# Second denominators next to the last kv product, output tiles 0 and 1 interleaved around them

## The chip, the cores and the metric

One core of a Trainium2 chip. The metric is the device time of one launch in microseconds (us).

Profiles name the engines in short: PE is TensorE (PEld its weight loads), DVE is VectorE, ACT is ScalarE, POOL is GpSimd and SP is SyncE, which issues most transfers. A bank here is one 128 x 512 f32 tile of the pools in PSUM, where this kernel's matmuls put their results.

## The reference, cut to what matters

```python
q, k, v = split(x @ wqkv)                        # 2048 rows, 32 heads of 32
pq, pk = phi(q), phi(k)                          # phi: t+1 where t > 0, else exp(t)
kv  = einsum("bhsd,bhse->bhde", pk, v)
z   = sum of pk over s
num = pq @ kv ;  den = pq @ z + 1e-6
a   = (num / den) @ wo
b   = x + (an expert's output, added to one row)
out = g * a + (1 - g) * b                        # g = sigmoid(x . gate_w)
```

The kernel multiplies kv with wo first (`m_sb`, a 1024 x 1024 matrix). It divides pq by its denominator in place, and then one product per output tile, pq times m_sb, gives a. Sixteen tiles of 128 rows are written.

## The kernel before

TensorE (`pe`) works in three array shapes at the place in question. Projections and output products use 128*128, the kv product with wo (`unit_M`, tiles `pm`) uses 32*32, and the denominators (`den_group`, tile `dps`) use 128*32.

```python
M_AFTER = {3: (0, 0), 6: (0, 1), 9: (1, 0), 12: (1, 1)}    # unit_M behind these projections
NORM_PER_T = [2, 3, 0, 2, 2, 2, 2, 2, 2, 2, 2, 1, 0, 0, 0, 0]

def den_group(pair):                     # denominators of 1024 rows: blocks j = 2*pair, 2*pair + 1
    pool, tag = (ps_work, "w") if pair == 0 else (ps_den, "d")
    dps = pool.tile([P, 512], F32, tag=tag, name="dps")
    ...                                  # 16 matmuls, lhsT = zc[:, g, :], rhs = pq_all[:, g, block j]
    act.activation(dn[:], dps[:], ACTF.Identity, bias=eps_t[:, 0:1])
    dve.reciprocal(rd[:], dn[:])
    for hh in range(4):                  # to rdp, half on SyncE's queue, half on GpSimd's
        eng = nc.sync if hh % 2 == 0 else nc.gpsimd
        eng.dma_start(out=rdp[pair][32 * hh : 32 * hh + 16, :], in_=rd[hh : P : 8, :])

def norm_step(n):                        # one of 32 normalisations: 8 g for each of 4 blocks j
    ...
    dve.stream_shuffle(rb[:], rd[:], [8 * (j % 2) + g] * 32)     # rb has four buffers
    nc.gpsimd.tensor_tensor(sl, sl, rb[:], op=ALU.mult)          # sl: pq_all, in place

def unit_M(hf, nh):                      # kv times wo, a quarter of m_sb
    pm = four_banks("pm")                # three banks of ps_den, one of ps_ffn
    ...                                  # 16 matmuls of 32*32, all side by side
    for r in range(4):
        eng = dve.tensor_copy if r == 3 else act.copy
        eng(m_sb[:, 4 * hf + r, 512 * nh : 512 * nh + 512], pm[r][:])
...
for i in range(len(q_units)):            # the last 13 projection units
    unit_Q(*q_units.popleft())
    if i in M_AFTER: unit_M(*M_AFTER[i])
    if i >= 3: norm_step(1)
phq.close()
for t in range(NT):                      # 16 output tiles, two column halves each
    ...                                  # load xt, xg = xt * (1 - gate) on ACT
    for c0, cw in cols:
        ...                              # 8 matmuls into ps (ps_work, four buffers)
        dve.scalar_tensor_tensor(ot[...], ps[...], gate[...], xg[...], op0=ALU.mult, op1=ALU.add)
    ...                                  # store ot
    if t == 0:
        rdB = den_group(1); normalise(rdB, 2); normalise(rdB, 3)
    norm_step(NORM_PER_T[t])
```

Of the kernel before, what the change touches and what calls it, by code (L numbers as in the profile page):

```python
# [13 lines left out]
BF = mybir.dt.bfloat16  # L14
F32 = mybir.dt.float32
I32 = mybir.dt.int32
U32 = mybir.dt.uint32
ALU = mybir.AluOpType
ACTF = mybir.ActivationFunctionType
# [3 lines left out]
P = 128  # L23
S = 2048
D = 1024
F = 3584
NT = S // P
KC = D // P
NG = D // P
# [7 lines left out]
KV_BEHIND = {(6, 3): 6}  # L37
FLUSH_AFTER = {(10, 2)}
ROW_STEPS = {4: (0, 1, 0, 1, 0, 1), 5: (0, 1, 0, 1, 1), 6: (0, 0, 0, 0, 1), 7: (0, 1, 1, 0, 1), 8: (0, 1, 0, 1, 1), 9: (1,)}
M_AFTER = {3: (0, 0), 6: (0, 1), 9: (1, 0), 12: (1, 1)}  # L40
DOWN_STEPS = {10: (0, 0, 0, 1, 1, 1), 11: (1, 1, 1, 1, 1), 12: (1, 1, 1, 1, 1), 13: (1, 1, 1, 1, 1), 14: (1, 1, 1, 1, 1), 15: (1, 1, 1, 1, 1)}
FFN_DEPTH = 10
NORM_PER_T = [2, 3, 0, 2, 2, 2, 2, 2, 2, 2, 2, 1, 0, 0, 0, 0]
# [3 lines left out]
def kernel(  # L47
# [13 lines left out]
    nc = tc.nc  # L61
    x2d = A_x.rearrange("b s d -> (b s) d")
    out2d = out.rearrange("b s d -> (b s) d")
# [6 lines left out]
    ps_work = ctx.enter_context(tc.tile_pool(name="ps_work", bufs=4, space=PSUM))  # L70
# [5 lines left out]
    strict = [True]  # L76
    strict_dve = [False]

    def in_order(engine, names, own=(False,)):
        last = [None]  # L80

        def wrap(fn):
            def call(*a, **k):
                inst = fn(*a, **k)  # L84
                if last[0] is not None and (strict[0] or own[0]):
                    tc.add_manual_dep(inst.ins, last[0].ins.name, NOSYNC, reason="program order on this engine")
                last[0] = inst
                return inst

            return call  # L90

        return SimpleNamespace(**{n: wrap(getattr(engine, n)) for n in names})

    pe = in_order(nc.tensor, ["matmul", "transpose"])
    dve = in_order(nc.vector, ["memset", "tensor_copy", "tensor_scalar", "tensor_scalar_add", "tensor_tensor", "scalar_tensor_tensor",
                               "reciprocal", "max", "max_index", "tensor_reduce", "stream_shuffle"], strict_dve)
    sp = in_order(nc.sync, ["dma_start", "dma_start_transpose"])
    act = in_order(nc.scalar, ["activation", "copy"])

    pq_all = keep.tile([P, NG, S], BF)  # L100
    gate = keep.tile([P, NT], F32)
    omg = keep.tile([P, NT], F32)
# [3 lines left out]
    xp = dram.tile([S, D], BF, name="xp")  # L106
# [144 lines left out]
    def unit_Q(g, j):  # L251
        ps = ps_work.tile([P, 512], F32, tag="w")
        for c in range(KC):
            pe.matmul(ps[:], lhsT=wq[:, c, g * P : (g + 1) * P], rhs=xT[:, c, 512 * j : 512 * j + 512],
                             start=(c == 0), stop=(c == KC - 1))
        phi_evac(ps[:], pq_all[:, g, 512 * j : 512 * j + 512])
# [337 lines left out]
    pb = ctx.enter_context(tc.tile_pool(name="pb", bufs=1))  # L594
    m_sb = pb.tile([P, NG, D], BF)
# [10 lines left out]
    ps_den = ctx.enter_context(tc.tile_pool(name="ps_den", bufs=3, space=PSUM))  # L606

    def den_group(pair):
        pool, tag = (ps_work, "w") if pair == 0 else (ps_den, "d")
        dps = pool.tile([P, 512], F32, tag=tag, name="dps")  # L610
        strict[0] = True
        for g0 in range(4):
            for jj in range(2):
                for g1 in range(2):
                    g = 4 * g1 + g0
                    j = 2 * pair + jj
                    q = 2 * jj + g1
                    pe.matmul(dps[32 * q : 32 * q + 32, :], lhsT=zc[:, g, :], rhs=pq_all[:, g, 512 * j : 512 * j + 512],
                                     start=(g0 == 0), stop=(g0 == 3), tile_position=(0, 32 * q))
        strict[0] = False  # L620
        dn = tmpb.tile([P, 512], F32, tag="dn")
        act.activation(dn[:], dps[:], ACTF.Identity, bias=eps_t[:, 0:1])
        rd = tmpb.tile([P, 512], F32, tag="rd")
        dve.reciprocal(rd[:], dn[:])
        for hh in range(4):
            eng = nc.sync if hh % 2 == 0 else nc.gpsimd
            eng.dma_start(out=rdp[pair][32 * hh : 32 * hh + 16, :], in_=rd[hh : P : 8, :])
        return rdp[pair]
# [3 lines left out]
    def normalise(rd, j):  # L632
        for g in range(NG):
            norm_units.append((rd, g, j))

    def norm_step(n):
        for _ in range(n):
            if not norm_units:
                return
            rd, g, j = norm_units.popleft()  # L640
            rb = tmpb.tile([P, 512], F32, tag="rb", bufs=4)
            dve.stream_shuffle(rb[:], rd[:], [8 * (j % 2) + g] * 32)
            sl = pq_all[:, g, 512 * j : 512 * j + 512]
            nc.gpsimd.tensor_tensor(sl, sl, rb[:], op=ALU.mult)  # L644

    def four_banks(name):
        banks = [ps_den.tile([P, 512], F32, tag="d", name=f"{name}{r}") for r in range(3)]
        banks.append(ps_ffn.tile([P, 512], F32, tag="f", name=f"{name}3"))
        return banks
# [14 lines left out]
    def unit_M(hf, nh):  # L664
        pm = four_banks("pm")
        for c in range(4):
            for r in range(4):
                pe.matmul(pm[r][32 * c : 32 * c + 32, :], lhsT=kvT[32 * r : 32 * r + 32, hf, c, :],
                          rhs=wo[2 * hf + c // 2][0][32 * r : 32 * r + 32, 1024 * (c % 2) + 512 * nh : 1024 * (c % 2) + 512 * nh + 512],
                          start=True, stop=True, tile_position=(32 * r, 32 * c))  # L670
# [4 lines that stand above are left out]
    rdA = den_group(0)  # L675
    strict[0] = True
    unit_kvT()
    strict[0] = False
    normalise(rdA, 0)
    normalise(rdA, 1)  # L680
    strict[0] = True
    for i in range(len(q_units)):
        unit_Q(*q_units.popleft())
        if i in M_AFTER:
            unit_M(*M_AFTER[i])
        if i >= 3:
            norm_step(1)
    strict[0] = False
    phq.close()

    fin = ctx.enter_context(tc.tile_pool(name="fin", bufs=3))
    for t in range(NT):
        xt = fin.tile([P, D], BF, tag="x3")
        nc.sync.dma_start(out=xt[:], in_=xp[t * P : (t + 1) * P, :])
        xg = fin.tile([P, D], F32, tag="xg3")
        strict[0] = True
        act.activation(xg[:], xt[:], ACTF.Copy, scale=omg[:, t : t + 1])
        strict[0] = False
        ot = fin.tile([P, D], BF, tag="o3")
        cols = [(0, 512), (512, 512)] if t < NT - 1 else [(0, 512), (512, 288), (800, 224)]  # L700
        for c0, cw in cols:
            ps = ps_work.tile([P, 512], F32, tag="w")
            for g in range(NG):
                pe.matmul(ps[:, 0:cw], lhsT=pq_all[:, g, t * P : (t + 1) * P], rhs=m_sb[:, g, c0 : c0 + cw],
                                 start=(g == 0), stop=(g == NG - 1))
            dve.scalar_tensor_tensor(ot[:, c0 : c0 + cw], ps[:, 0:cw], gate[:, t : t + 1],
                                           xg[:, c0 : c0 + cw], op0=ALU.mult, op1=ALU.add)
            if t == NT - 1:
                nc.sync.dma_start(out=out2d[t * P : (t + 1) * P, c0 : c0 + cw], in_=ot[:, c0 : c0 + cw])
        if t < NT - 1:  # L710
            nc.sync.dma_start(out=out2d[t * P : (t + 1) * P, :], in_=ot[:])
        if t == 0:
            rdB = den_group(1)
            normalise(rdB, 2)
            normalise(rdB, 3)
        norm_step(NORM_PER_T[t])


# [28 lines left out]
```

## Time and profile before

| | before |
|---|---|
| time, median of 6 runs | 248.58 us (248.30 to 248.77) |
| profiled span | 246.6 us |
| TensorE busy | 241.8 us (98%) |
| first projection behind the third `pm` to the last matmul, start to start | 61.92 us |
| start of the last matmul to the end of the span | 3.82 us |

The chain of waits that ended last, in order of time (start, duration, engine, tile), finishes like this in the kernel before:

```profile
186.22 0.36 PE pm L84 x16
186.59 3.56 PE ps L84 x16
190.15 0.98 PE dps L84 x16
191.12 51.94 PE ps L84 x248
243.06 0.02 issue
243.09 0.45 DVE ot L84
```

Each row begins where the one above ends. TensorE is the chain, and the last output evacuation on VectorE (DVE) closes it.

### The profile page before, as it was taken

How to read it: one execution, taken by the hardware profiler on the slowest of the kernel's cores; microseconds unless marked ns; L12 is line 12 of the kernel's file. 1: busy time of each engine (PE TensorE's matmuls, PEld its weight loads, DVE VectorE, ACT ScalarE, POOL GpSimd, SP SyncE). 2: the span in 40 equal slices, each digit the busy share in tenths (PEclk: the TensorE clock that was granted, in tenths of full speed). 3: DMA queues.
4: the chain of work that ended last, by engine and by line, in shares of the span. 5: the costliest groups of instructions: out<-in, count | busy, mean ns of one | idle time of the engine just before them, and what ended most of it. 6: DMA issues, size and time to landing. Idle time of an engine off the chain costs nothing.

```text
span 246.6 us, 4896 instructions
## 1 busy us (share of the span) xinstructions
PE 241.8 (98%) x1926; PEld 124.6 (51%) x1926; DVE 172.6 (70%) x264; ACT 127.5 (52%) x215; POOL 52.6 (21%) x100
## 2 busy tenths in 40 slices
PE   8999999999999999999999999999999999999994
PEld 4466756654565554554555555444443444444442
DVE  1053124379975899835999999996789999954442
ACT  3095343355554565545576455668887633333300
POOL 6000000400000000000003400101666689950000
PEclk9999999999999999999999999999999999999999
DMA  6999994399968994499549690000003664464122
GB/s 215 341 239 196 274 390 139 108 350 335 265 192 251 353 314 120 146 319 386 188 157 535 212 287 16 3 4 21 0 3 128 202 185 147 153 190 166 48 85 86
DMA packets 46311, 47.78 MB, mean 194 GB/s; under 512 B 16776, under 2 KB 35472, under 8 KB 46224
## 3 DMA queue, kind: packets, MB, share of 16 engines
q1 hardware_dynamic: 45648, 46.28, 60.7%
q0 software_dynamic: 608, 1.19, 1.6%
q8 instruction: 15, 0.25, 0.4%
q14 instruction: 8, 0.07, 0.1%
q10 hardware_dynamic: 32, 0.00, 0.0%
HBM read 39.33 MB, written 8.39 MB: 194 GB/s over the span
## 4 chain that ended last, share of the span: by engine, by line
PE 96%; DMA 2%; SPq 1%; DVE 0%; issue 0%
PE ps L84 89%; PE first L84 3%; PE kvacc L84 2%; DMA wkv<-in_A_wqkv_dram 2%; PE dps L84 1%; PE red L84 1%; PE pm L84 1%; SPq L84 1%; PE yps L84 0%; DVE ot L84 0%; PE pt L84 0%; PE hps L84 0%; PE rps L84 0%; PE xs_ps L84 0%
## 5 line engine op out<-in xcount | busy, mean ns | idle before, releaser
L84 PE MATMUL ps<-wkv,xT 128*128 128x352 bf16 (+2 forms) x608 | 106.5, 334 | 0.0
L84 PEld LDWEIGHTS <-xT 128*128 128x128 bf16 x640 | 62.2, 98 | 49.7 <-issue 0.9
L84 ACT ACTIVATE u<-ps 128x512 f32<-128x512 f32 x60 | 35.9, 598 | 45.4 <-PE ps L84 45.2
L84 PE MATMUL ps<-xT,wq 128*128 128x512 bf16 x256 | 58.1, 379 | 0.0
L84 PE MATMUL ps<-m_sb,pq_all 128*128 128x512 bf16 (+2 forms) x264 | 55.6, 373 | 0.0
L84 ACT ACTIVATE e<-u 128x512 f32<-128x512 f32 x64 | 40.3, 630 | 2.0
L84 PEld LDWEIGHTS <-pq_all 128*128 128x128 bf16 x264 | 25.7, 98 | 29.9 <-issue 0.7
L644 POOL TENSOR_TENSOR pq_all<-pq_all,rb 128x512 bf16<-128x512 bf16 x32 | 36.4, 1166 | 12.1 <-DVE rb L84 11.7
L84 PEld LDWEIGHTS <-wq 128*128 128x128 bf16 x256 | 24.6, 98 | 28.1 <-issue 0.7
L84 DVE SCALAR_TENSOR_TENSOR gacc<-wt,hcol,gacc 128x1024 f32<-128x1024 bf16 x27 | 34.5, 1278 | 0.4
L84 DVE SCALAR_TENSOR_TENSOR ot<-ps,gate,xg 128x512 bf16<-128x512 f32 (+2 forms) x33 | 24.0, 736 | 14.2 <-PE ps L84 14.1
L84 DVE SCALAR_TENSOR_TENSOR gacc<-wt,xs_f,gacc 128x2048 f32<-128x2048 bf16 x14 | 32.8, 2345 | 0.2
L84 ACT ACTIVATE xg<-xt,omg 128x1024 f32<-128x1024 bf16 x16 | 18.1, 1146 | 26.9 <-DVE ot L84 25.9
L84 DVE SCALAR_TENSOR_TENSOR pq_all<-ps,e 128x512 bf16<-128x512 f32 x32 | 21.9, 687 | 11.7 <-ACT e L84 11.7
L84 DVE SCALAR_TENSOR_TENSOR pk<-ps,e 128x512 bf16<-128x512 f32 x28 | 18.9, 684 | 10.0 <-ACT e L84 10.0
L84 DVE STREAM_SHUFFLE rb<-rdp 128x512 f32<-128x512 f32 x32 | 22.7, 747 | 0.0
L84 ACT CAST vt<-ps 128x352 bf16<-128x352 f32 x32 | 14.3, 453 | 11.4 <-PE ps L84 11.1
L214 POOL MEMSET vt<- 128x22 bf16 x16 | 3.8, 445 | 56.1 <-PE kvacc L84 55.9
L480 POOL DMA_DIRECT2D wt<-in_A_wo_dram x8 | 4.3, 542 | 32.1 <-PE ps L84 29.5
L84 ACT CAST vc<-ps 128x320 bf16<-128x320 f32 x16 | 6.5, 428 | 7.3 <-PE ps L84 7.3
L84 DVE COPY rg<-ps 128x2 f32<-128x2 f32 x16 | 2.5, 159 | 10.2 <-ACT vc L84 10.1
L356 POOL DMA_DIRECT2D xs<-in_A_x_dram x1 | 0.7, 711 | 39.3 <-DVE sig L84 39.3
(100 smaller groups left out, 93.9 us busy)
## 6 DMA issues: line engine op xcount, KB each, us to landing
wt<-in_B_w_down_dram SPq DMA_DIRECT2D x14, 512.0 KB, 4.0
wt<-in_B_w_gate_dram SPq DMA_DIRECT2D x8, 512.0 KB, 7.5
wt<-in_B_w_up_dram SPq DMA_DIRECT2D x8, 512.0 KB, 7.2
xt<-xp SPq DMA_DIRECT2D x16, 256.0 KB, 2.6
out_dram<-ot SPq DMA_DIRECT2D x15, 256.0 KB, 2.0
wt<-in_B_w_gate_dram SPq DMA_DIRECT2D x8, 384.0 KB, 7.1
wt<-in_B_w_up_dram SPq DMA_DIRECT2D x8, 384.0 KB, 6.8
wkv<-in_A_wqkv_dram SPq DMA_DIRECT2D x8, 256.0 KB, 4.3
```

Of the source, the lines that this page charges most:

```text
L84: inst = fn(*a, **k)
L214: nc.gpsimd.memset(vt_t[t][:, :, 32:33], 1.0)
L356: nc.gpsimd.dma_start(out=xs8[:], in_=x2d[bass.ds(idx_val, 1), :].rearrange("o (c p) -> (o c) p", p=P))
L480: ld = eng.dma_start(out=wt[32 * r : 32 * r + 32, :].rearrange("p (c n) -> p c n", c=2), in_=wo_v[k // 2, r][:, 2 * (k % 2) : 2 * (k % 2) ...
L644: nc.gpsimd.tensor_tensor(sl, sl, rb[:], op=ALU.mult)
```

## The change

Its intent is to save a change of array shape on TensorE. The denominators of the second half move right behind the last `unit_M`, so that the two small shapes are adjacent. Tile 0's first output half runs ahead of both, to give VectorE time for the last projection unit, which those denominators need. Tile 1's first half goes between the halves of tile 0. For this, tile 0's x is loaded and scaled earlier, into buffers of its own, and the denominators use a bank of `ps_work`.

```diff
-M_AFTER = {3: (0, 0), 6: (0, 1), 9: (1, 0), 12: (1, 1)}
+M_AFTER = {3: (0, 0), 6: (0, 1), 9: (1, 0)}
 ...
-        pool, tag = (ps_work, "w") if pair == 0 else (ps_den, "d")
-        dps = pool.tile([P, 512], F32, tag=tag, name="dps")
+        dps = ps_work.tile([P, 512], F32, tag="w", name="dps")
 ...
+    xt0 = final_load(0, pb, 1)
     for i in range(len(q_units)):
         unit_Q(*q_units.popleft())
         ...
+        if i == 10:
+            final_scale(0, xt0)
+    final_cols(0, 0, 512)
+    unit_M(1, 1)
+    rdB = den_group(1)
+    normalise(rdB, 2)
+    normalise(rdB, 3)
     phq.close()
 ...
+        if t == 1:
+            final_cols(1, 0, 512)
+            final_cols(0, 512, 512)
+            nc.sync.dma_start(out=out2d[0:P, :], in_=ots[0][:])
+            norm_step(NORM_PER_T[0])
 ...
-        if t == 0:
-            rdB = den_group(1)
-            normalise(rdB, 2)
-            normalise(rdB, 3)
```

(`final_load`, `final_scale` and `final_cols` are the load, the scaling and the product with evacuation of the old loop, cut into functions.)

More of the change, by code (lines that the diff above doesn't have):

```diff
@@ L680, with final_load, final_scale, final_cols @@
     normalise(rdA, 1)
+    xgs, ots = {}, {}
+    def final_load(t, pool, bufs):
+        xt = pool.tile([P, D], BF, tag="x3", bufs=bufs)
+        nc.sync.dma_start(out=xt[:], in_=xp[t * P : (t + 1) * P, :])
+        xgs[t] = pool.tile([P, D], F32, tag="xg3", name=f"xg{t}", bufs=bufs)
+        ots[t] = pool.tile([P, D], BF, tag="o3", name=f"ot{t}", bufs=bufs)
+        return xt
+    def final_scale(t, xt):
+        act.activation(xgs[t][:], xt[:], ACTF.Copy, scale=omg[:, t : t + 1])
+    def final_cols(t, c0, cw):
+        ps = ps_work.tile([P, 512], F32, tag="w")
+        for g in range(NG):
+            pe.matmul(ps[:, 0:cw], lhsT=pq_all[:, g, t * P : (t + 1) * P], rhs=m_sb[:, g, c0 : c0 + cw],
+                             start=(g == 0), stop=(g == NG - 1))
+        dve.scalar_tensor_tensor(ots[t][:, c0 : c0 + cw], ps[:, 0:cw], gate[:, t : t + 1],
+                                       xgs[t][:, c0 : c0 + cw], op0=ALU.mult, op1=ALU.add)
+    xt0 = final_load(0, pb, 1)
     strict[0] = True
@@ L687 @@
             norm_step(1)
-    strict[0] = False
+        if i == 10:
[5 more added lines that the diff above has]
+    normalise(rdB, 3)
     phq.close()
     fin = ctx.enter_context(tc.tile_pool(name="fin", bufs=3))
-    for t in range(NT):
-        xt = fin.tile([P, D], BF, tag="x3")
-        nc.sync.dma_start(out=xt[:], in_=xp[t * P : (t + 1) * P, :])
-        xg = fin.tile([P, D], F32, tag="xg3")
+    for t in range(1, NT):
+        xt = final_load(t, fin, 3)
         strict[0] = True
-        act.activation(xg[:], xt[:], ACTF.Copy, scale=omg[:, t : t + 1])
-        strict[0] = False
-        ot = fin.tile([P, D], BF, tag="o3")
-        cols = [(0, 512), (512, 512)] if t < NT - 1 else [(0, 512), (512, 288), (800, 224)]
-        for c0, cw in cols:
-            ps = ps_work.tile([P, 512], F32, tag="w")
-            for g in range(NG):
-                pe.matmul(ps[:, 0:cw], lhsT=pq_all[:, g, t * P : (t + 1) * P], rhs=m_sb[:, g, c0 : c0 + cw],
-                                 start=(g == 0), stop=(g == NG - 1))
-            dve.scalar_tensor_tensor(ot[:, c0 : c0 + cw], ps[:, 0:cw], gate[:, t : t + 1],
-                                           xg[:, c0 : c0 + cw], op0=ALU.mult, op1=ALU.add)
-            if t == NT - 1:
-                nc.sync.dma_start(out=out2d[t * P : (t + 1) * P, c0 : c0 + cw], in_=ot[:, c0 : c0 + cw])
-        if t < NT - 1:
-            nc.sync.dma_start(out=out2d[t * P : (t + 1) * P, :], in_=ot[:])
-        if t == 0:
-            rdB = den_group(1)
-            normalise(rdB, 2)
-            normalise(rdB, 3)
+        final_scale(t, xt)
+        if t == 1:
[3 more added lines that the diff above has]
+            norm_step(NORM_PER_T[0])
+        strict[0] = t == 1
+        cols = [(0, 512), (512, 512)] if t < NT - 1 else [(0, 512), (512, 288), (800, 224)]
+        for c0, cw in cols[1 if t == 1 else 0 :]:
+            final_cols(t, c0, cw)
+            if t == NT - 1:
+                nc.sync.dma_start(out=out2d[t * P : (t + 1) * P, c0 : c0 + cw], in_=ots[t][:, c0 : c0 + cw])
+        if t < NT - 1:
+            nc.sync.dma_start(out=out2d[t * P : (t + 1) * P, :], in_=ots[t][:])
+        strict[0] = False
         norm_step(NORM_PER_T[t])
```

## The prediction

> **What bounds the kernel now.** I read the page first: its head, its slices and the chain of work that ended last.
>
> ```profile
> PE 241.8 (98%) x1926; PEld 124.6 (51%) x1926; DVE 172.6 (70%) x264; ACT 127.5 (52%) x215; POOL 52.6 (21%) x100
> PE   8999999999999999999999999999999999999994
> POOL 6000000400000000000003400101666689950000
> PE 96%; DMA 2%; SPq 1%; DVE 0%; issue 0%
> ```
>
> TensorE (PE) is the bound from end to end: it has work in every slice, and 96% of the last chain is PE. So a change can gain only by taking TensorE time away, and it loses whatever it makes TensorE wait. No other engine's busy time matters by itself. After the last matmul only some 3.6 us follow (span 246.6 less 243.0), which the change leaves alone.
>
> The second view is the timeline of PE around the place that the diff touches (start, duration, engine, line, operation, operands).
>
> ```profile
> 174.85 0.43 PE L84 MATMUL pm<-wt,kvT 32*32 32x512 bf16 x16
> 175.22 5.35 PE L84 MATMUL ps<-xT,wq 128*128 128x512 bf16 x24
> 180.50 0.43 PE L84 MATMUL pm<-wt,kvT 32*32 32x512 bf16 x16
> ...
> 186.15 0.43 PE L84 MATMUL pm<-wt,kvT 32*32 32x512 bf16 x16
> 186.52 3.63 PE L84 MATMUL ps<-m_sb,pq_all 128*128 128x512 bf16 x16
> 190.08 1.05 PE L84 MATMUL dps<-pq_all,zc 128*32 128x512 bf16 x16
> 191.06 51.99 PE L84 MATMUL ps<-m_sb,pq_all 128*128 128x512 bf16 x248
> ```
>
> Each row starts as the one before it ends, so there are no stalls. But each row change is also a change of array shape: 128*128 for the projections, 32*32 for the kv product with wo (pm), 128*32 for the denominators (dps). In steady flow a 512-column matmul starts every 0.216 us (the outputs of a tile follow each other at 218.90 and 222.35 in the DVE timeline: 3.45 us for 16). Read record by record, the last projection before pm starts at 185.843 and the first pm at 186.153: 0.310 us in place of 0.216. The same step is 0.309 before dps and 0.322 after it. So **a change of shape costs about 0.10 us**. Check: pm to pm is 5.65 us, less 24 x 0.216 = 0.47; two changes (0.2), one wave of sixteen concurrent matmuls (0.22) and their issue (0.05) give 0.47.
>
> **What the Trainium skill says.** "TensorEngine Tiling (Array Packing)", Key Properties: changing the tiling mode drains the TensorE. The trace agrees, with the 0.31 in place of 0.216 us above; the page gives no figure. "TensorE: Matmul & The Clock Gate", the table at its head: ScalarE, VectorE and GpSimdE work off strict FIFOs, while TensorE may only pull weight loads forward. The trace agrees: GpSimd's issue of the `rdp` transfer at 197.15 waited for the reciprocal on VectorE, and no multiplication behind it went ahead. This is the rule on which my main doubt rests. "Perfetto Trace Analysis", Optimization Strategy: interleave regimes with different contended engines; that is what moving the denominators does, but here TensorE bounds both sides.
>
> **The change, part by part.**
>
> 1. *Order on TensorE.* Before: Q, pm, tile 0 (both halves), dps, tile 1: four changes of shape. After: Q, first half of tile 0, pm, dps, first half of tile 1, second of tile 0, second of tile 1: three. The instruction count is unchanged (the order listing has 3809 PE rows in both). Gain: one change, **0.10 us**. A change between 32*32 and 128*32 is not free: at 161.6 to 161.9 the trace has one from dps to the small transposing products, also 0.31 us from last start to first.
>
> 2. *Early readiness of tile 0.* Its first half now starts at 185.843 + 0.216 = 186.06, not 186.52. Its eighth weight load needs the eighth normalisation on POOL, which ran from 185.99 to 187.16; the load is due at 186.06 + 6 x 0.216 = 187.35. It fits by 0.2 us. The scaled x for tile 0 (ACT, 1.15 us) is moved between two Q evacuations and pushes the last one: its u starts at some 186.8 instead of 186.26, so pq_all of the last unit is written by 188.06 + 0.69 = 188.75. On PE: first half to 187.57 (start of its last matmul), pm 187.88, dps 188.23, its fourth wave 188.88. Only that wave needs the last unit. It fits, by 0.1 us.
>
> 3. *Denominators off their own banks.* dps moves into the rotating four ps buffers. The tightest reuse that I find is tile 3's second half, whose buffer is free at some 197.5 for a start at 199.6. No stall.
>
> 4. *The second denominators become ready earlier, but fewer normalisations are ahead of them.* Here lies the cost. Before, GpSimd did 14 multiplications, then issued its half of the `rdp` transfer, then 18; after, 10 and 22 (order listing). Tiles 4 to 7 need multiplications 9 to 16. These are the rows of before:
>
> ```profile
> 189.56 5.67 POOL L644 TENSOR_TENSOR pq_all<-pq_all,rb 128x512 bf16<-128x512 bf16 x5 [1.15 <-DVE rb L84]
> 197.15 1.03 POOL L627 DMA_DIRECT2D rdp<-rd  x2 [1.92 <-issue]
> 198.57 1.15 POOL L644 TENSOR_TENSOR pq_all<-pq_all,rb 128x512 bf16<-128x512 bf16 x1 [0.40 <-DVE rb L84]
> 199.91 19.28 POOL L644 TENSOR_TENSOR pq_all<-pq_all,rb 128x512 bf16<-128x512 bf16 x17 [0.18 <-PE ps L84]
> ...
> 193.27 3.34 DVE L84 RECIPROCAL rd<-dn 128x512 f32<-128x512 f32 x1
> ```
>
> Number 16 is the first of the seventeen: done at 201.07. Tile 4 starts at 191.06 + 6 x 1.727 = 201.42 and loads number 16's block at about 202.7, so there were 1.6 us of slack.
>
> After: VectorE writes the last Q unit from 188.06, then a shuffle, the first output half, the copy of pm and then the reciprocal, at steps of 0.61, 0.65, 0.65 and 0.61: it starts near 190.6 and ends R = 193.95 (3.34 us). dn is ready before, at 190.4, since ACT now does it ahead of the scaled x. GpSimd's transfers follow (0.54 + 1.03 as before), while VectorE does two outputs and the first shuffle: multiplication 11 begins at R + 1.96 (198.57 less 196.61 before), the rest follow at 1.12 us, and number 16 ends at R + 1.96 + 5 x 1.12 + 1.17 = R + 8.73 = **202.7**. TensorE: first half of tile 1 at 188.88 + 0.32 = 189.20, seven halves to tile 4 at 201.3, its eighth weight load at 202.6. So 1.6 us of slack become about minus 0.1: a stall of **0 to 0.3 us**, 0.1 if I take the numbers as they stand. Later groups have room: multiplications 17 to 24 end near 211.7 for tile 8 at 215.
>
> Sum: -0.10 + 0.1 = about 0; against 248.6 I put **248.5**, leaning slightly to the gain because the stall may not happen at all.
>
> **The rivals.**
>
> *A: the gain alone.* GpSimd is just in time and one shape change is saved: 248.5. For it: every estimate in part 4 is within its own error of the need. If also the drain between pm and dps overlaps, 248.4.
>
> *B: GpSimd becomes the wait.* If the reciprocal starts 0.5 us later than I reckon (VectorE's queue, or dn behind the copies of pm), tile 4 waits some 0.6 us and TensorE never gets it back: 249.1. For it: zero slack, strict FIFO. Against it: the chain is short and all its steps are rows of the trace.
>
> *C: VectorE becomes the wait.* It is idle little from 191 to 205 (27 instructions fill 13.9 us), and during the 3.34 us of the reciprocal TensorE fills two more buffers. With four buffers it got through this before; the reciprocal now comes one half earlier in the sequence. 248.6 to 249 at worst.
>
> *D: the hoisted load of tile 0's x delays the first `rdp` transfers*, which share its queue. 256 KB land in 2.6 us (DMA issues of the page), issued near 164.5; the first shuffle is at 171.81, with 3 us to spare. Nothing.
>
> **Range and chances.** The terms are -0.1 and 0 to +0.6, and the three runs of before spread over 0.5 us by themselves. So 248.0 to 249.1. Two per cent would be 5 us, which no term approaches: same 0.98.
>
> **What would show it right or wrong.** Right: in the PE timeline three changes of shape between Q and the end, each 0.31 us, and dps starting near 188.2. The reciprocal starts at 190.6 and the second `rdp` issue on POOL near 194.5. The sixteenth multiplication ends near 202.7, and tile 4's last weight load of its first half (the eighth) waits for POOL by at most 0.3 us. Wrong: an idle gap on PE over 0.3 us there, a gap before dps's last wave (ACT pushed too far), or a wait of a ps matmul for DVE in tiles 2 to 4. The prediction as a whole fails if such a gap exceeds half a microsecond, or if changes of shape differ much from 0.1 us.

## The result

248.29 us (median of 6 runs, 248.06 to 248.48) against 248.58 us before. The ratio is 0.9990, with a 95% interval of 0.9977 to 1.0002. Ratios here are the mean time of one kernel's fast runs over that of the other's of the same rounds, so not quite the ratio of the medians. A repeat with five rounds gave 248.22 against 248.51 us, ratio 0.9983 (0.9968 to 0.9998): a small gain. Its middle, 0.42 us, is larger than the 0.1 us that the prediction reckoned with before any stall, but the interval, 0.05 to 0.80 us, doesn't exclude 0.1.

The page after, same lines as in the prediction:

```profile
PE 241.8 (98%) x1926; PEld 124.7 (51%) x1926; DVE 172.4 (70%) x264; ACT 127.4 (52%) x215; POOL 52.5 (21%) x100
PE   7999999999999999999999999999999999999994
POOL 6000000300000000000003400101566399980000
PE 96%; DMA 2%; SPq 1%; DVE 0%; issue 0%
```

Little changed at this resolution, except that GpSimd (POOL) has a hole in slice 32 (the digit 3 between 6 and 9) and is busier than before in the slices behind it. The timeline of PE after, around the changed place:

```profile
181.01 0.43 PE L84 MATMUL pm<-wt,kvT 32*32 32x512 bf16 x16
181.38 5.35 PE L84 MATMUL ps<-xT,wq 128*128 128x512 bf16 x24
186.57 1.89 PE L84 MATMUL ps<-m_sb,pq_all 128*128 128x512 bf16 x8
188.39 0.43 PE L84 MATMUL pm<-wt,kvT 32*32 32x512 bf16 x16
188.75 1.05 PE L84 MATMUL dps<-pq_all,zc 128*32 128x512 bf16 x16
189.73 16.58 PE L84 MATMUL ps<-m_sb,pq_all 128*128 128x512 bf16 x76
```

The reader sees three changes of shape behind the last projections in place of four, and still no gap. This trace runs 0.51 us later than the one before (181.38 against 180.87 for the projection behind the third pm), because the loads at the start of the program took longer (the first matmul of the tiles `ps<-wkv` starts at 13.46 us, before at 12.97); that differs from run to run, whatever the kernel. Record by record, the **stretch**, from the first projection behind the third `pm` to the last matmul, start to start, is 61.815 us, before 61.922: **0.107 us less**.

The timeline of POOL and of DVE's reciprocal after:

```profile
188.62 2.40 POOL L643 TENSOR_TENSOR pq_all<-pq_all,rb 128x512 bf16<-128x512 bf16 x2 [0.96 <-DVE rb L84]
194.98 1.02 POOL L626 DMA_DIRECT2D rdp<-rd  x2 [3.96 <-issue]
196.41 12.38 POOL L643 TENSOR_TENSOR pq_all<-pq_all,rb 128x512 bf16<-128x512 bf16 x11 [0.41 <-DVE rb L84]
...
191.09 3.35 DVE L84 RECIPROCAL rd<-dn 128x512 f32<-128x512 f32 x1
```

GpSimd now stands still for 3.96 us before its half of the transfer, where before it was 1.92. (The view names no releaser, but the reciprocal, which the transfer needs, ended 0.54 us before it.) That is the price named in part 4 of the prediction. The sixteenth multiplication ends at 203.18 and the weight load that needs it starts at 203.23, 0.10 us later than the rhythm of the loads before it (202.69, 202.91) asks for. But its matmul begins on time at 203.34: a load is normally issued a whole step of 0.216 us ahead, and here that distance shrank to 0.11. **The stall is zero, with about 0.1 us to spare.**

The **end**, from the start of the last matmul to the end of the span, is the surprise: 3.44 us, before 3.82. The change saved 0.107 us in the stretch and 0.383 us in the end, 0.49 us in all; the five rounds of the repeat measured 0.0017 x 248.5 = 0.42 us.

### The profile page after: what moved, and what is told of

It reads as the page before. It is cut to its first block, busy times and chain, and to the rows that moved or that the text cites. A ratio compares the mean times of both kernels' runs of the same rounds, so it can differ in the third digit from the quotient of the medians.

```text
span 246.6 us, 4895 instructions
## 1 busy us (share of the span) xinstructions
PE 241.8 (98%) x1926; PEld 124.7 (51%) x1926; DVE 172.4 (70%) x264; ACT 127.4 (52%) x215; POOL 52.5 (21%) x100
## 4 chain that ended last, share of the span: by engine, by line
PE 96%; DMA 2%; SPq 1%; DVE 0%; issue 0%
PE ps L84 89%; PE first L84 3%; PE kvacc L84 2%; DMA wkv<-in_A_wqkv_dram 2%; PE red L84 1%; PE dps L84 1%; PE pm L84 1%; SPq L84 1%; PE yps L84 0%; DVE ot L84 0%; PE pt L84 0%; PE hps L84 0%; PE rps L84 0%; PE xs_ps L84 0%
## 5 line engine op out<-in xcount | busy, mean ns | idle before, releaser
L84 DVE SCALAR_TENSOR_TENSOR ot<-ps,gate,xg 128x512 bf16<-128x512 f32 (+2 forms) x33 | 23.7, 726 | 13.7 <-PE ps L84 12.3
L84 DVE SCALAR_TENSOR_TENSOR pk<-first,e 128x512 bf16<-128x512 f32 x4 | 2.8, 692 | 9.6 <-ACT e L84 9.6
```

Source lines behind the costliest of these rows:

```text
L84: inst = fn(*a, **k)
```

## The experiments

My theories: (1) the stretch got shorter by one change of shape and by nothing else; (2) GpSimd serves tile 4 just in time; (3) tile 0's first half ahead of the rest, the bank and the interleaving are there to avoid stalls. Each rival is in the expectation of its run. All gave correct results except one, which is told.

| run | stretch, us | end, us | sum against before | time and ratio to before |
|---|---|---|---|---|
| before | 61.92 | 3.82 | | |
| changed | 61.82 | 3.44 | -0.49 | 248.29, 0.9990 (0.9977 to 1.0002) |
| repeat | 61.81 | 3.44 | -0.49 | 248.22, 0.9983 (0.9968 to 0.9998) |
| between | 61.92 | 3.76 | -0.06 | 248.84, 1.0005 (0.9985 to 1.0025) |
| twelve | 61.82 | 3.44 | -0.49 | 248.24, 0.9980 (0.9962 to 0.9998) |
| straight | 61.82 | 3.44 | -0.49 | 247.97, 0.9979 (0.9961 to 0.9996) |
| uncovered | 63.30 | 3.81 | +1.37 | 250.44, 1.0060 (1.0044 to 1.0077) |
| denbank | 62.61 | 3.77 | +0.63 | 249.53, 1.0031 (1.0014 to 1.0048) |
| ninefull | 62.84 | 3.44 | +0.54 | 249.37, 1.0031 (1.0016 to 1.0046) |
| shape32 | 67.04 | 3.44 | +4.73 | 253.57, 1.0185 (1.0168 to 1.0202) |
| shape128 | 62.93 | 3.44 | +0.62 | 249.81, 1.0036 (1.0016 to 1.0056) |
| beforeplus | 61.92 | 3.25 | -0.57 | 247.94, 0.9977 (0.9963 to 0.9991) |
| afterminus | 61.81 | 3.97 | +0.04 | 248.84, 1.0009 (0.9995 to 1.0024) |

The fourth column is the sum of the two lengths less 65.74 us. In every row it lies inside the interval of the ratio times 248.5 to 248.9 us. So these two lengths account for what the rounds show. What scatters in single runs is the start: in the fourteen profiles the first matmul of the tiles `ps<-wkv` starts at 12.8 to 13.7 us.

### The changed kernel again

No edit.

> The changed kernel again, for a tighter interval. Theory: the gain is one change of array shape, 0.10 us; from the first projection after the third pm to the start of the last matmul 61.82 us, as in the first profile of it (before: 61.92). Ratio to before 0.9996, 248.4 to 248.5. Rival: the medians so far, 0.29 us apart, are the true gain, and something outside this stretch also became shorter: ratio 0.9988.

Stretch 61.814 us, the same to 0.001 us. The ratio of 0.9983 leans to the rival but doesn't decide, since its interval just reaches the theory's 0.9996. The trace decides: the end is 3.44 us again, 0.38 less than before, so something outside the stretch became shorter as well.

### Four changes of shape again

```diff
-    final_cols(0, 0, 512)
     unit_M(1, 1)
+    final_cols(0, 0, 512)
     rdB = den_group(1)
```

> The changed kernel with the first half of tile 0 put between pm and the denominators: the shapes change four times again, all else (banks, earlier load, interleaved tile 1, ten normalisations ahead) stays. Theory: 0.10 us more than the changed kernel, the stretch from the third pm to the last matmul 61.92 us, and no stall. Rival, that the gain comes from the other parts of the change: 61.82 us as in the changed kernel.

The timeline of PE in this run:

```profile
186.39 0.43 PE L84 MATMUL pm<-wt,kvT 32*32 32x512 bf16 x16
186.76 1.90 PE L84 MATMUL ps<-m_sb,pq_all 128*128 128x512 bf16 x8
188.59 1.05 PE L84 MATMUL dps<-pq_all,zc 128*32 128x512 bf16 x16
189.57 16.79 PE L84 MATMUL ps<-m_sb,pq_all 128*128 128x512 bf16 x75
```

One more row, that is one more change of shape, and the stretch is 61.922 us: the whole of the gain in the stretch is gone, and exactly it. The other parts of the change contribute nothing there.

### The cost of a change of shape by itself

```diff
         for c0, cw in cols[1 if t == 1 else 0 :]:
+            if 5 <= t < 15:
+                ...                                      # one bank that nobody reads
+                pe.matmul(dum[0:32, 0:128], lhsT=ident[0:32, 0:32], rhs=m_sb[0:32, 0, 0:128],
+                          start=True, stop=True, tile_position=(0, 0))     # shape32
+                pe.matmul(dum[:, 0:128], lhsT=ident[:], rhs=m_sb[:, 0, 0:128],
+                          start=True, stop=True)                           # or shape128
             final_cols(t, c0, cw)
```

> The changed kernel with twenty needless 128-column matmuls of shape 32*32 (into a bank that nobody reads; the result stays right) ahead of the output halves of tiles 5 to 14: forty more changes of shape. Theory: each change costs 0.10 us and each needless matmul 0.05: 20 x (0.09 + 0.16) = 5.0 us more than the changed kernel, time 253.3, unless other engines' waits hide some. Rival, that the change of shape is cheap here and the 0.31 us step belongs to its neighbourhood: 1.1 to 1.5 us more, like its twin of full shape.

> The same with twenty needless 128-column matmuls of full shape 128*128: no change of shape. Theory: only the matmul itself, 0.05 to 0.11 us each (128 columns at 0.216 us per 512, or a weight load of 98 ns that isn't hidden): 1.1 to 2.2 us more than the changed kernel, time 249.4 to 250.5. The difference to the twin of 32*32 shape is the cost of forty changes of shape. Rival: equal to the twin.

The timelines of PE, first of shape32, then of shape128:

```profile
215.40 0.22 PE L84 MATMUL dum<-m_sb,ident 32*32 32x128 bf16 x1
215.55 1.90 PE L84 MATMUL ps<-m_sb,pq_all 128*128 128x512 bf16 x8
217.38 0.23 PE L84 MATMUL dum<-m_sb,ident 32*32 32x128 bf16 x1
```

```profile
216.32 0.22 PE L84 MATMUL dum<-m_sb,ident 128*128 128x128 bf16 x1
216.37 1.89 PE L84 MATMUL ps<-m_sb,pq_all 128*128 128x512 bf16 x8
218.10 0.22 PE L84 MATMUL dum<-m_sb,ident 128*128 128x128 bf16 x1
```

From one needless matmul to the next it is 1.99 us in the first (1.987 to 1.989, record by record) and 1.78 us in the second. The stretches are 67.04 and 62.93 us: forty changes of shape cost 4.11 us, **0.103 us each**, and the twenty matmuls by themselves 1.12 us, 0.056 each. The stretch of shape32 is 5.22 us above that of the changed kernel, where I expected 5.0. So the 0.107 us that the change saves is the ordinary price of one change of shape. In shape128 the weight load beside the short matmul cost nothing extra, the lower end of what I had expected.

### Is GpSimd just in time?

Two kernels move the number of normalisations ahead of the second denominators, which is ten in the changed kernel. The first:

```diff
         if i >= 3:
-            norm_step(1)
+            norm_step(2 if i in (6, 9) else 1)
```

> The changed kernel with twelve normalisations ahead of the second denominators instead of ten. Theory: in the changed kernel tile 4 is served just in time and does not stall, so more slack wins nothing: the stretch 61.82 us, the sixteenth multiplication done about 2.2 us earlier (near 201.0). Rival, that a stall hides at tile 4: up to 0.1 us less.

The sixteenth multiplication ended 19.56 us after the start of the stretch instead of 21.80, and the stretch stayed at 61.815 us. No stall hid at tile 4.

The second has one normalisation fewer ahead:

```diff
-        if i >= 3:
+        if 3 <= i < 12:
             norm_step(1)
```

> The changed kernel with nine normalisations ahead of the second denominators instead of ten. Theory: GpSimd is just in time, so one multiplication of 1.12 us more behind its wait for the reciprocal shows up whole: tile 4's eighth weight load waits 1.0 to 1.1 us, stretch 62.9 us, time 249.4. Rival, that there is slack of half a microsecond or more that the trace does not show: 61.8 to 62.4 us.

This run's output was wrong, by my mistake: the list of normalisations per tile was one short, so the thirty-second never ran. Its stretch was 62.83 us. It was mended by one more in the list for tile 11:

> The run with nine normalisations ahead, mended (the first left out the thirty-second at the end and so gave a wrong result): one more in the list for tile 11. Theory: as the first showed, a stall of 1.02 us at tile 4, stretch 62.83 us, now with a right result; ratio to before 1.002 to 1.003. Rival, that the missing instruction mattered for the stall: another stretch.

The result is right and the stretch is 62.84 us. Its timeline of POOL and then of PE:

```profile
188.57 1.17 POOL L643 TENSOR_TENSOR pq_all<-pq_all,rb 128x512 bf16<-128x512 bf16 x1 [0.95 <-DVE rb L84]
194.93 1.02 POOL L626 DMA_DIRECT2D rdp<-rd  x2 [5.20 <-issue]
...
189.69 13.89 PE L84 MATMUL ps<-m_sb,pq_all 128*128 128x512 bf16 x61
204.31 1.90 PE L84 MATMUL ps<-m_sb,pq_all 128*128 128x512 bf16 x8 [0.73 <-POOL pq_all L643]
```

The sixteenth multiplication ends 1.12 us later than in the changed kernel, and TensorE loses 1.03 us. So the changed kernel has about 0.1 us to spare. Record by record, behind the wait the load starts at 204.305 and its matmul at 204.310: a matmul's recorded start needs its load only 0.005 us ahead, so the 0.11 us that were left in the changed kernel were room to use.

### What the first half of tile 0, the bank and the interleaving are for

```diff
-    final_cols(0, 0, 512)
     unit_M(1, 1)
     rdB = den_group(1)
+    final_cols(0, 0, 512)                # between strict[0] = True and False, cut here
```

> The changed kernel with tile 0's first half behind the denominators instead of ahead of pm: the adjacency alone, three changes of shape, nothing between the last projection and pm. Theory: the denominators' last wave needs the last unit of pq_all, which VectorE wrote at 189.12 in the changed kernel's trace, and would be due at about 187.7: a stall of 1.5 us, stretch from the third pm to the last matmul 63.3 us, time 249.8. Rival, that only the number of changes of shape counts: 61.82 us and 248.4.

The timeline of PE:

```profile
187.25 1.33 PE L84 MATMUL dps<-pq_all,zc 128*32 128x512 bf16 x15
189.40 0.38 PE L84 MATMUL dps<-pq_all,zc 128*32 128x512 bf16 x1 [0.82 <-DVE pq_all L84]
189.71 16.58 PE L84 MATMUL ps<-m_sb,pq_all 128*128 128x512 bf16 x76
```

The sixteenth denominator matmul starts 1.2 us after the fifteenth and waits for DVE's write of pq_all, as expected (a wait of 0.27 us comes one wave earlier too). The stretch is 63.297 us against 63.3 expected. Adjacency alone loses 1.48 us against the changed kernel, to save 0.11; against the kernel before it loses 1.38.

```diff
-        dps = ps_work.tile([P, 512], F32, tag="w", name="dps")
+        pool, tag = (ps_work, "w") if pair == 0 else (ps_den, "d")
+        dps = pool.tile([P, 512], F32, tag=tag, name="dps")
```

> The changed kernel with the second denominators in the bank pool of before (shared with pm). Theory: they then wait until ACT has copied the first bank of pm, about 0.57 us after 188.91 in the changed kernel's trace, so they start near 189.5 instead of 188.75: 0.75 us more, stretch 62.55 us, time 249.0. Rival, that the bank pool doesn't matter: 61.82 us.

The timeline of PE:

```profile
188.25 0.43 PE L84 MATMUL pm<-wt,kvT 32*32 32x512 bf16 x16
189.41 1.05 PE L84 MATMUL dps<-pq_all,zc 128*32 128x512 bf16 x16 [0.72 <-ACT m_sb L84]
```

The wait for ACT's copy of pm is there and the stretch is 62.61 us (expected 62.55). The adjacency needs a bank that pm doesn't hold.

```diff
-            final_cols(1, 0, 512)
             final_cols(0, 512, 512)
+            final_cols(1, 0, 512)
```

> The changed kernel with tile 0's second half directly behind the denominators, ahead of tile 1's first (no interleaving of tile 1). Its last matmul needs the last copy of pm, which ends 1.28 us after the denominators' first matmul's start plus 0.98 (191.01 against 189.73 in the trace); it is due 1.51 us after. Theory: fits by 0.2 us, so 61.82 us still. Rival, that the interleaving is needed: a stall of 0.1 to 0.3 us at that matmul.

Stretch 61.815 us: the interleaving of tile 1 isn't needed at these times. By the estimate in the expectation it adds margin for the last copy of pm, which no run measured.

### The end

The ends in the table aren't random. Leaving aside the last two rows, which were built to move the end, they are 3.44 us in every kernel with 215 records on SyncE and 3.76 to 3.82 in before, between, uncovered and denbank, which have 213 or 214, though stores and last matmul are the same. (So the times of between, uncovered and denbank hold some 0.3 to 0.4 us that their theories don't speak of.) These are SyncE's last records, read from the traces (number of the record on SyncE, start in us after the last matmul's start, the semaphores that it waits for; a drain is an instruction that follows the list of waits):

```
before (213 records, end 3.82)            changed (215 records, end 3.44)
204  1.71  S105, S112                     206  1.71  S105, S112
205  2.37  S106, S111  last landing       207  2.36  S106, S111  last landing
206  2.46  S107, S109                     208  2.44  S107, S109
207  2.85  S108, S110                     209  2.50  S108, S110
208  2.92  drain                          210  2.57  drain
```

The last store lands at 2.35 and 2.34 us in the two. Then SyncE goes down the same list of waits, all long fulfilled, at steps of 0.06 to 0.10 us. In the kernel before one step, from record 206 to 207, takes 0.39 us. In the changed kernel record 206 comes before the wait for the last landing, where such a pause costs nothing. In between and denbank (214 records) and in uncovered (213) the long step, 0.39 us, is from 206 to 207 too. What differs is the number of records ahead of it: the count of semaphore waits before SyncE's transfers happens to be two higher in the changed kernel. The theory is a pause of 0.32 us (0.39 less an ordinary step) at SyncE's record 206, wherever that falls; the other 0.06 us of the difference between the two ends are smaller steps in the same list. It was tested from both sides.

Before, with more records, and nothing else:

```diff
+        if t in (9, 10):
+            nc.sync.dma_start(out=out2d[t * P : (t + 1) * P, 0:512], in_=ot[:, 0:512])
+            nc.sync.dma_start(out=out2d[t * P : (t + 1) * P, 512:D], in_=ot[:, 512:D])
-        if t < NT - 1:
+        elif t < NT - 1:
             nc.sync.dma_start(out=out2d[t * P : (t + 1) * P, :], in_=ot[:])
```

> The kernel before with the stores of tiles 9 and 10 split into two halves each, nothing else: three more records in SyncE's stream (216 instead of 213), the order of all other engines untouched. Theory: SyncE pauses for a third of a microsecond at its record 206 in every kernel; before, that is behind its wait for the last landing and lengthens the end, in the changed kernel (215 records) it falls into that wait and is hidden. So here, without any of the change, the time from the last matmul's start to the end falls from 3.82 to 3.44 us, the stretch from the third pm to the last matmul stays at 61.92, and the time falls by 0.3 to 0.4 us (ratio 0.9985). Rival, that the shorter end comes from the change itself: 3.82 and ratio 1.000.

The changed kernel, with fewer:

```diff
-        nc.sync.dma_start(out=xt[:], in_=xp[t * P : (t + 1) * P, :])
+        (nc.gpsimd if t == 0 else nc.sync).dma_start(out=xt[:], in_=xp[t * P : (t + 1) * P, :])
```

> The changed kernel with the early load of tile 0's x issued on GpSimd's queue: three fewer records in SyncE's stream (212 instead of 215), order of TensorE, VectorE and ACT untouched. Theory: the pause at SyncE's record 206 comes out from behind the wait for the last landing: the end grows from 3.44 to 3.75-3.85 us, the stretch stays at 61.82, and the time is 248.5 to 248.6, that is 0.1 us under before (ratio 0.9996), the gain of the one change of shape alone. Rival: 3.44 and ratio 0.9983 as in the repeat.

```
beforeplus (216 records, end 3.25)        afterminus (212 records, end 3.97)
206  1.50  S104, S113                     203  2.37  S105, S112  last landing
207  1.89  S105, S112                     204  2.42  S106, S111
208  1.97  S106, S111                     205  2.51  S107, S109
209  2.03  S107, S109                     206  2.59  S108, S110
210  2.31  S108, S110  last landing       207  2.98  drain
211  2.38  drain                          208  3.17  drain
```

The long step is at record 206 again, 0.39 us in both. It is hidden in the first, whose order on the other engines is that of before, and exposed in the second, which has the whole change. The times follow: the kernel before gains 0.0023 x 248.5 = 0.57 us without the change (95%: 0.22 to 0.92), and the changed kernel no longer shows a gain (ratio 1.0009; the interval, 0.9995 to 1.0024, just holds the 0.9996 expected). The stretches stayed at 61.92 and 61.81 us.

Both ends missed the size that I had put down (3.44 and 3.75 to 3.85). In beforeplus the last store uses another semaphore, which stands last in SyncE's list, so two waits fewer follow the landing (0.14 us), which itself came 0.05 us earlier. In afterminus three waits follow the landing instead of two (0.09 us), and a second long step follows the first (0.19 us at 207, where it was 0.07 to 0.10 elsewhere), which no run takes apart.

What the pause is, no run shows either. The Trainium skill, "Runtime: NRT & Kernel Launch", Instruction fetch mechanics, says that instructions are fetched in blocks of 256 and that crossing a block is mostly hidden. A fixed place in the stream would fit this. The DMA records give a hint: in all fourteen traces a packet of the kind "instruction" (8 KB, queue 14) starts 1.01 to 1.31 us after SyncE's record 206 (1.03 in before, 1.04 in beforeplus and 1.03 in afterminus), although that record lies anywhere from 1.50 to 2.59 us behind the last matmul. So a fetch of instructions goes with this place in SyncE's stream. It starts when the pause of 0.39 us is over, and no run moved the one without the other: that the fetch, or the crossing that calls for it, makes the pause is likely and not shown.

## Why the prediction was right, and where it wasn't

**The time** was right: 248.5 said, 248.29 and 248.22 measured. But a part of the agreement is luck, since two terms of 0.1 and 0.4 us were off in the sum and the range covered them.

**Part 1, one change of shape, 0.10 us**: right. The stretch fell by 0.107 us, came back with a fourth change, and forty added ones gave 0.103 each. (One step was misread: from the last dps to the next ps it is 0.312 us in the trace, not 0.322. The pages have 1926 matmuls in both kernels.) That the change between 32*32 and 128*32 isn't free is right too: 0.314 us from the last pm's start to the first dps.

**Part 2, tile 0 early**: right, no wait there. The denominators' last wave was covered, and the uncovered run shows what the cover is worth (1.48 us).

**Part 3, buffers**: right; no reuse of ps stalled. The prediction didn't say what happens without the new bank, which the run denbank showed.

**Part 4, GpSimd just in time**: the chain was right to within 0.1 us. Shifted by the 0.51 us between the traces, the reciprocal started at 190.58 (said 190.6), the transfer was issued at 194.47 (194.5) and the sixteenth multiplication ended at 202.67 (202.7). The stall put at 0.1 us was zero. The mis-sized term is what a late weight load costs: I let it delay its matmul from the first moment, but it may be late by nearly the whole step of 0.216 us by which it is issued ahead (0.10 us were used, 0.11 left). The strict FIFO on which the prediction rests its doubt wasn't tested: the multiplication behind the transfer had no data to go ahead with, since VectorE began its shuffle only behind the reciprocal (197.76 us before, 195.60 after). What held it back in these traces is the order on VectorE.

**Rivals**: A came true in the stretch, without its addition that the drain between pm and dps might overlap. B is what one multiplication fewer brings on (ninefull), and C and D didn't show.

**The step that failed** is a sentence in the first part: "After the last matmul only some 3.6 us follow (span 246.6 less 243.0), which the change leaves alone." The end, counted from the last matmul's start (3.82 us before), changed by 0.38 us, more than three times the intended gain. The change didn't mean to touch it: by altering how many waits stand in SyncE's stream, it moved a pause out of the exposed end. So the gain, as the traces show it, is one part design and three and a half parts accident of position, and the kernel before gets the accidental part by splitting two stores.

## What to carry to other kernels

Where TensorE is busy throughout, count its changes of array shape: each cost 0.10 us here, and putting small shapes side by side saves one, if the data of the second are ready and its bank is free. Covering both cost more thought than the gain: a missing cover lost 1.5 us, a missing bank 0.8. When a measured gain is larger than the mechanism explains, look at the ends of the program, record by record, before you credit the change: an engine's closing list of waits was on the path here, and its length and place depended on things that nobody meant to alter. A version with both (the order of straight and the stores of beforeplus) suggests itself and wasn't run.

## What the Trainium skill lacked or had wrong

- "TensorEngine Tiling (Array Packing)", Key Properties, states the drain at a change of tiling mode without a figure. The runs show 0.103 us per change (4.11 us for forty between 128*128 and 32*32), and 0.098 us for the one from 32*32 to 128*32 (0.314 less 0.216).
- "Runtime: NRT & Kernel Launch", Instruction fetch mechanics, calls a crossing of an instruction block mostly hidden. If the pause at SyncE's record 206 is one, which is not shown, it is 0.32 us and stands in full where it follows the last landing; an instruction packet of 8 KB starts 1.01 to 1.31 us after that record in all fourteen traces. No page that I read mentions such a pause.
- No page that I read says that the closing waits on SyncE are on the path: here 0.06 to 0.09 us for each of those behind the last landing, so that the place of the last store's semaphore in the list was worth 0.14 us.
